# Token loads by single heads, scatters one at a time, and router logits in two places, in a convolution and expert-routing kernel

## The chip, the core and the metric

The kernel runs on one core of a Trainium2 chip. A core has five engines with queues of their own: TensorE (matmuls; the profile keeps its weight loads apart as PEld), VectorE (DVE), ScalarE (ACT), GpSimd (POOL) and SyncE (SP, which only issues transfers). Each engine works through its queue in program order and waits on semaphores where it needs another's result. Sixteen DMA engines carry all transfers, which SyncE, ScalarE and GpSimd issue. Matmuls write to PSUM banks, which ScalarE and VectorE empty.

The metric is the device time of one execution in microseconds (us), the median of several runs. Lower is better.

## What is computed

A causal convolution of seven taps, with softmax-normalised weights for each of eight heads of 24 channels, is followed by a mixture of eight experts. Each token's expert is the argmax of its logits, unless a local gate keeps the expert of the token before it, so the choice runs along the sequence. There are 8 sequences of 3584 tokens with 192 channels; an expert is 192 to 1024 to 192 with a relu. All is in float32.

```python
w = softmax(weight)                                   # [8 heads, 7 taps]
x = einsum('hk,bskhg->bshg', w, windows(x_pad))       # 24 channels to a head
logits = x @ w_gate                                   # [B, S, 8]
local_gate = sigmoid(x @ w_local)
for b in range(B):
    prev_e = -1
    for s in range(S):
        fresh_e = argmax(logits[b, s])
        e = fresh_e if s == 0 or local_gate[b, s] < 0.5 else prev_e
        prev_e = e
        p = softmax(logits[b, s])
        out[b, s] = p[e] * (relu(x[b, s] @ w1[e]) @ w2[e])
```

## The kernel before

**The pipeline.** Tokens are taken in groups. The groups are convolved, routed (logits, argmax, the run along the sequence, each token's place among the tokens of its expert) and scattered: each token's row of 195 words goes by an indirect DMA of GpSimd to its slot in DRAM (`slots`), where the tokens of one expert stand together. A scatter takes 128 rows. While later groups are on their way, *blocks* of tokens that are sure to be full are loaded back (`xg`), transposed, multiplied by their expert's two matrices and sent to the output by another indirect DMA (line 1198). Blocks of one tile (128 tokens) come first, 51 of them (numbers 0 to 50), then 20 pairs (51 to 70), then 31 quads of four tiles (71 to 101), then 14 single ones. Groups 0 and 1 go a special way at the start (`wide`, `wide_route`). Groups 2 and 3 hold 1792 tokens, the later ones 3584.

**Token loads and the filter.** A group is convolved in *units*, `(g, qq)`, of `DH = D // XQ` channels. With `XQ = 4` a unit is two heads. `load_x` (148) fetches a unit to one of three places in `x_all` for the small groups, or one of two for the large ones. ScalarE issues that transfer, except the first three, which SyncE issues. `tap` (417) multiplies one head's first tap on ScalarE (line 426) and `conv` (453) adds the other six on VectorE (line 464, six instructions a head). `taps` (438), called once in `output`, issues the next load if it is within the depth (3 or 2 units), then taps ahead for this unit and the next; `ready` (429) says whether the next may begin: its load was issued in an earlier block, and the groups whose buffer it will use have been routed and scattered.

**Order of the work.** The order of every engine is written out by hand (`manual_schedule`). The loop over blocks (1358) emits, for block i: `hidden` (first matrix, lines 1086 and 1090), or for quads `seven` (a scheme with seven products, line 1136), the next block's transposes (`turn_out` 1043, `turn_in` 1055), a `step`, `output` (second matrix, line 1178, its emptying on ScalarE 1186 and VectorE 1193, and the store 1198), and for smaller blocks a further `step`. `step(time, bank)` (1240) takes so much of the VectorE work that is waiting, from the routing (`route` 688) or else the filter. `ensure` (1304) issues the loads of rows up to three blocks ahead; it returns early where the group isn't routed and scattered, and in the last block before the need it works that off first. On SyncE's queue a load of rows waits for the scatters of its group, and the weights' loads stand in the same queue.

**Scatters.** `to_put` holds the scatters of routed groups; `put` (865) issues one, behind a given instruction. `more` (885) issues a second where the list is long, `puts_by` (890) both. They hang behind relus (1090), the copies of the transposes (1064) and copies in `seven`.

**Logits.** `logits` (642) transposes a group's rows on VectorE (652) and multiplies them by the gate's weights in 48 matmuls of both halves for every 14 tiles (line 665), with a yield "half" in the middle, in a PSUM bank that `step` was given. Copies by ScalarE (669) empty it. `step` stops the routing at "half" unless `whole` is set, which only `ensure` does.

**Quads.** `combine_w` (1097) makes four sums of the next quad's first matrix on GpSimd (1102 to 1105).

Of the kernel before, what the change touches and what calls it, by code (L numbers as in the profile page):

```python
# [17 lines left out]
P = 128  # L18
# [16 lines left out]
XQ = 4  # L35
# [74 lines left out]
def kernel(  # L110
# [32 lines left out]
    x_all = xs.tile([P, 2 * NX, DH], F32, name="x_sb")  # L143
# [4 lines left out]
    def load_x(u, queue=None):  # L148
        g, qq = UNITS[u]
        n, skip = (NT, g % PER * PT) if g < EARLY else (NS, 0)  # L150
        at = (u + 2) % 3 * (NT + HALO) if g < EARLY else (u + 1) % 2 * NX
        x_sb = x_all[:, at:at + n + HALO, :]
        src = x[g // PER, qq]
        win = bass.AP(tensor=src.tensor, offset=src.offset + skip * DH,
                      ap=[[n * DH, P], [1, (n + HALO) * DH]])
        (queue or nc.scalar).dma_start(out=x_sb.rearrange("p t d -> p (t d)"), in_=win)
        x_in[u] = x_sb
        x_at[u] = -1 if queue else st["block"]
# [256 lines left out]
    EACH = H // XQ  # L415

    def tap(u, j):

        if (u, j) in begun:
            return  # L420
        begun.add((u, j))
        g, qq = UNITS[u]
        if (qq, j) == (0, 0):
            got[g] = rows_in(g)
        h, n = qq * EACH + j, NT if g < EARLY else NS
        nc.scalar.activation(got[g][:, :, Y0 + h * GS:Y0 + (h + 1) * GS],  # L426
                             x_in[u][:, :n, j * GS:(j + 1) * GS], Act.Copy, scale=c[:, h, 0:1])

    def ready(u):

        if u >= len(UNITS) or u not in x_in or st["block"] <= x_at[u]:
            return False
        last = (UNITS[u][0] // PER - 3) * PER + 1
        if last < 0:
            last = UNITS[u][0] // PER - 2
        return st["routed"] >= last and not any(p[0] <= last for p in to_put)

    def taps(most):

        u = len(x_in)  # L440
        if u < len(UNITS):
            depth = 3 if UNITS[u][0] < EARLY else 2
            if u - depth <= st["unit"] - (st["cgen"] is not None):
                load_x(u)
        for u in (st["unit"], st["unit"] + 1):
            if u > st["unit"] and not ready(u):
                return
            for j in range(EACH):
                if u >= 0 and (u, j) not in begun and most:
                    tap(u, j)  # L450
                    most -= 1

    def conv(u):
        g, qq = UNITS[u]
        n = NT if g < EARLY else NS
        tap(u, 0)
        yield 0
        for j in range(EACH):
            h = qq * EACH + j
            cols = got[g][:, :, Y0 + h * GS:Y0 + (h + 1) * GS]  # L460
            if j + 1 < EACH:
                tap(u, j + 1)
            for k in range(1, KC):
                nc.vector.scalar_tensor_tensor(cols, x_in[u][:, k:k + n, j * GS:(j + 1) * GS],  # L464
                                               c[:, h, k:k + 1], cols, Alu.mult, Alu.add)
                yield 0.6 if n == NT else 1.0
# [418 lines left out]
    def more(behind, n=KT):  # L885

        if len(to_put) > (NT if n < KT else NT // 2):
            put(behind)

    def puts_by(behind):  # L890
        put(behind)
        more(behind)

# [181 lines left out]
    def hidden(n, wb, xT, shares=(1, 1)):  # L1075
# [3 lines left out]
        for two in range(2):  # L1079
# [11 lines left out]
            for _ in range(shares[two] if n == 2 else (0, sum(shares))[two]):  # L1091
                put(relu)
            if two and (n == 2 or st["block"] % 2):
                more(relu, n)
        return [hT]

    def combine_w(wb):


        wt = hp.tile([P, 3, 2 * P], F32, name="wt")  # L1100
        b11, b12, b21, b22 = [wb[:, k * 2 * P:(k + 1) * 2 * P] for k in range(4)]
        nc.gpsimd.tensor_tensor(wt[:, 1, :], b22, b12, op=Alu.subtract)  # L1102
        nc.gpsimd.tensor_tensor(b12, b12, b11, op=Alu.subtract)
        nc.gpsimd.tensor_tensor(wt[:, 0, :], b22, b12, op=Alu.subtract)
        nc.gpsimd.tensor_tensor(wt[:, 2, :], b21, wt[:, 0, :], op=Alu.subtract)
        return wt
# [13 lines left out]
    def seven(wb, wt, xT, xc, turn_next, weights_next):  # L1120
# [12 lines left out]
        def times(to, a, b, first=False):  # L1133
            for j in range(2):
                for half, rows in halves():
                    nc.tensor.matmul(to[:, half, j, :], lhsT=b[rows, j * P:(j + 1) * P],  # L1136
                                     rhs=a[rows, :], start=(first and j == 0), stop=True,
                                     skip_group_check=True)

        times(xb, a11, b11, True)  # L1140
        puts_by(nc.scalar.copy(h11, xb))
        times(yb, s1, t1, True)
        times(yb, a23, b32)
        puts_by(nc.scalar.copy(h22, yb))
        times(xb, s2, t2)
        nc.scalar.copy(h12, xb)
        times(wbk, a12, b21, True)
# [4 lines left out]
        times(xb, s3, t3)  # L1152
# [3 lines left out]
        times(yb, s5, b32)  # L1156
# [3 lines left out]
        times(xb, a23, b31)  # L1160
        nc.vector.tensor_tensor(h12, yb, h12, op=Alu.add)
        puts_by(nc.scalar.activation(h12, h12, Act.Relu))
# [3 lines left out]
    def output(n, wb, xg, hT, rows_next=None):  # L1166

        for part, h in enumerate(hT):
# [3 lines left out]
            for two in range(2):  # L1172
                for k in range(m):
                    for m_ in range(4):
                        side, j = m_ // 2, m_ % 2
                        f = side * 4 + two * 2 + j
                        for half, rows in halves():
                            nc.tensor.matmul(yps[:, half, k * D:(k + 1) * D],  # L1178
                                             lhsT=h[two][rows, side, j, k * P:(k + 1) * P],
                                             rhs=wb[rows, WA + f * D:WA + (f + 1) * D],  # L1180
                                             start=(two == 0 and m_ == 0 and k == 0),
                                             stop=(f == FK - 1), skip_group_check=True)
# [5 lines left out]
            if rows_next and part == 0:  # L1188
                taps(min(n, 2))
            step((1.3 if n > 1 or st["block"] else 0) if n < KT else SIDE[2 + part],  # L1190
                 wps_p if n < KT or part == 0 else None)
# [21 lines left out]
          "bank": None, "due": False, "over": 0}  # L1213
# [26 lines left out]
    def step(time, bank=None, whole=False):  # L1240

        start_route()
        start_conv()
        go = st["rgen"] is not None and not (st["due"] and bank is None)
        st["bank"], st["due"] = bank, st["due"] and not go
        time += st["over"]
        while time > 0:
# [11 lines left out]
            elif c == "half":  # L1259
                go = whole  # L1260
# [25 lines left out]
    load_x(0, nc.sync)  # L1286
    load_x(1, nc.sync)
    load_x(2, nc.sync)
# [15 lines left out]
    def ensure(i):  # L1304

        for j in range(len(xgs) + i, min(i + AHEAD + 1, len(blocks))):
            g = blocks[j][3]
            while st["routed"] < g or any(p[0] <= g for p in to_put):
                if j > i + (2 if blocks[i][1] == 1 else 1):
                    return  # L1310
                step(4.2, wps_p, True)
# [19 lines left out]
    puts_behind(mark["lt", 1], 3)  # L1331
# [7 lines left out]
    gather(1, ya, picks[1], range(9))  # L1339
    next(route1)  # L1340
    puts_behind(mark["nf", 1], 2)
    puts_behind(mark["rs", 1], 4)
    step(1.8)
    at = turn_out(blocks[0][1], xgs[0])
    xT, _ = turn_in(blocks[0][1], at)
    gather(1, ya, picks[1], range(9, NB))
    next(route1)
    step(2.4)
    xgs[1] = gathered(picks[1])
# [8 lines left out]
    for i, (_, n, _, _) in enumerate(blocks):  # L1358
# [8 lines left out]
        def weights_next():  # L1367
            return combine_w(wbs[i + 1]) if n_next == KT else None
# [3 lines left out]
        else:  # L1372
            hT = hidden(n, wbs[i], xT, (1, 1) if i else (0, 0))
            wt = weights_next()
            at = turn_next()
        if n_next:
            xT, copied = turn_in(n_next, at)
            if n == KT or (len(to_put) > NT // 2 and n == 2):
                puts_by(copied)
        xcs = []  # L1380

        def rows_next():
            if n_next == KT and not xcs:
                xcs.append(combine_x(xT))

        if n == 2:
            rows_next()
        step(2.4 if i == 0 else {1: 2.3, 2: 4.7, 4: SIDE[1]}[n], zps_p if n == KT else xps_p)
        output(n, wbs.pop(i), xgs.pop(i), hT, rows_next)
# [94 lines left out]
```

## Time and profile before

| | us |
|---|---|
| timed runs | 1338.44, 1326.51, 1338.53 (median 1338.44) |
| the profiled execution | 1377.82 |
| its span in the profile, first to last instruction | 1376.1 |
| TensorE busy in the span | 1307.0 |
| VectorE / ScalarE / GpSimd busy | 824.0 / 688.0 / 622.2 |
| mean granted TensorE clock | 0.984 of full |

How to read it. A group of instructions is named by its line, its engine and what it writes and reads: `PE L1178 MATMUL ps<-wb,h` is a matmul of line 1178 into a bank `ps`. In a timeline a row gives start and length in us, then the group, and in brackets how long the engine was idle before it and what ended that idle time. "issue" and "remote" there mean that the profile shows nothing that it waited for, or something outside the core's records. In the chain of waits, the instruction that ended last is followed back to what released it, again and again. The list of waits gives total us, number, and the longest. DMA share is the mean busy share of the sixteen DMA engines.

The stages in the span are: the start up to 54, single blocks up to about 381, pairs up to about 610, quads up to 1290, then the last single blocks. Two tables of the page show the DMA load by 40 slices of 34.4 us:

```
DMA  5898899899787676674334442423342332332583
GB/s 179 327 342 312 322 352 331 316 316 349 295 327 257 216 242 235 213 282 142 124 139 145 144 139 83 151 100 115 134 151 88 133 128 93 128 119 85 189 315 114
```

### The profile page before, as it was taken

Reading aid. Unit: us, or ns where it says so; the run is one execution under the profiler, and the core shown is the slowest. Engines: PE = TensorE matmul, PEld = TensorE weight load, DVE = VectorE, ACT = ScalarE, POOL = GpSimd, SP = SyncE. Lnnn points to the kernel's source line nnn. Section 1 sums busy time; section 2 is a strip of 40 time slices with the busy share of each in tenths; the row PEclk is TensorE's granted clock in tenths of the full one; section 3 lists DMA queues with packets and bytes.
Section 4 is the critical chain, followed back from the end, with each engine's and each line's share of the span. In section 5 each row is a group of like instructions: output and inputs, shape, how many; then the busy total and the mean of one; then the engine's idle time right before and its main releaser. Section 6 shows DMA issues by size and latency. Waiting matters only on the chain.

```text
span 1376.1 us, 40772 instructions
## 1 busy us (share of the span) xinstructions
PE 1307.0 (95%) x16674; PEld 1256.1 (91%) x16674; DVE 824.0 (60%) x1891; ACT 688.0 (50%) x1402; POOL 622.2 (45%) x650
## 2 busy tenths in 40 slices
PE   9899889998899999998999999998999999999997
PEld 7889888998899998987998999888999999999997
DVE  6878687787787887887777755763333333343100
ACT  5355445554444444545564545443545645655453
POOL 4444444156366374476546643465543333333111
PEclk9999999999999999999999999999999999999999
DMA  5898899899787676674334442423342332332583
GB/s 179 327 342 312 322 352 331 316 316 349 295 327 257 216 242 235 213 282 142 124 139 145 144 139 83 151 100 115 134 151 88 133 128 93 128 119 85 189 315 114
DMA packets 62788, 281.17 MB, mean 204 GB/s; under 512 B 12032, under 2 KB 30647, under 8 KB 48258
## 3 DMA queue, kind: packets, MB, share of 16 engines
q1 hardware_dynamic: 36096, 210.76, 43.0%
q0 software_dynamic: 22320, 45.22, 9.0%
q10 hardware_dynamic: 4178, 22.51, 4.6%
q8 instruction: 134, 2.20, 0.6%
q14 instruction: 60, 0.49, 0.1%
HBM read 232.85 MB, written 46.07 MB: 203 GB/s over the span
## 4 chain that ended last, share of the span: by engine, by line
PE 85%; DVE 5%; DMA 5%; issue 3%; POOL 1%; ACT 1%; another core or an unknown queue 0%; DVEq 0%; POOLq 0%; ACTq 0%; SPq 0%
PE ps L1178 42%; PE ps L1136 21%; PE ps L1086 17%; DMA x_sb<-in_x_dram 3%; PE ps L665 2%; PE ps L400 2%; DVE y_sb L464 1%; DMA slots<-y_sb,posi 1%; DVE h L1153 1%; PE hps L249 1%; POOL slots L872 1%; DMA out_dram<-o_sb,xg 0%; PE hps L194 0%; ACT h L1090 0%
## 5 line engine op out<-in xcount | busy, mean ns | idle before, releaser
L1178 PE MATMUL ps<-wb,h 64*128 64x192 f32 x7328 | 641.4, 328 | 27.6 <-ACT h L1090 12.6
L1178 PEld LDWEIGHTS ps<-wb,h 64*128 64x128 f32 x7328 | 609.5, 189 | 37.7 <-ACT h L1090 19.9
L1198 POOL DMA_INDIRECT out_dram<-o_sb,xg x229 | 251.9, 1100 | 470.4 <-DVE o_sb L1193 397.3
L464 DVE SCALAR_TENSOR_TENSOR y_sb<-x_sb,c,y_sb 128x672 f32<-128x672 f32 (+1 forms) x384 | 322.7, 848 | 35.2 <-ACT y_sb L426 21.4
L872 POOL DMA_INDIRECT slots<-y_sb,posi x228 | 253.8, 1113 | 120.5 <-issue 52.8
L1086 PE MATMUL ps<-xT,wb 64*128 64x128 f32 (+1 forms) x4080 | 299.3, 298 | 3.5 <-issue 2.1
L1193 DVE SCALAR_TENSOR_TENSOR o_sb<-ps,xg,o_sb 128x192 f32<-128x192 f32 x229 | 87.7, 413 | 353.2 <-ACT o_sb L1186 346.8
L1086 PEld LDWEIGHTS ps<-xT,wb 64*128 64x128 f32 x4080 | 281.5, 188 | 16.1 <-issue 7.2
L1186 ACT ACTIVATE o_sb<-ps,xg 128x192 f32<-128x192 f32 x229 | 87.3, 418 | 332.0 <-PE ps L1178 286.9
L1090 ACT ACTIVATE h<-ps 128x256 f32<-128x256 f32 (+1 forms) x340 | 127.5, 431 | 152.3 <-PE ps L1086 109.5
L1064 ACT COPY xT<-ps 128x128 f32<-128x128 f32 (+2 forms) x464 | 194.3, 419 | 10.5 <-issue 3.2
L1136 PE MATMUL ps<-xT,wb 64*128 64x256 f32 x1488 | 182.8, 379 | 1.1 <-issue 1.0
L1136 PEld LDWEIGHTS ps<-xT,wb 64*128 64x128 f32 x1488 | 157.9, 189 | 7.6 <-issue 2.9
L1150 DVE TENSOR_TENSOR h<-ps,h 128x1024 f32<-128x1024 f32 x31 | 37.9, 1223 | 92.8 <-PE ps L1136 90.0
L1102 POOL TENSOR_TENSOR wt<-wb 128x256 f32<-128x256 f32 x31 | 23.5, 758 | 129.1 <-issue 129.1
L1136 PE MATMUL ps<-xc,wt 64*128 64x256 f32 x496 | 67.7, 381 | 1.6 <-issue 1.6
L1151 ACT ACTIVATE h<-h 128x1024 f32<-128x1024 f32 x31 | 32.8, 1057 | 69.4 <-DVE h L1150 50.2
L400 PE MATMUL ps<-ident,xg 64*64 64x64 f32 (+1 forms) x916 | 51.2, 220 | 11.0 <-DVE h L1150 4.7
L426 ACT ACTIVATE y_sb<-x_sb,c 128x672 f32<-128x672 f32 (+1 forms) x64 | 48.9, 793 | 24.2 <-DMA x_sb<-in_x_dram 24.1
L1136 PE MATMUL ps<-xc,wb 64*128 64x256 f32 x496 | 60.0, 376 | 0.0
L400 PEld LDWEIGHTS ps<-ident,xg 64*64 64x64 f32 (+1 forms) x916 | 46.3, 125 | 14.9 <-issue 6.6
L1136 PEld LDWEIGHTS ps<-xc,wt 64*128 64x128 f32 x496 | 53.3, 189 | 4.1 <-issue 2.4
(266 smaller groups left out, 975.1 us busy)
## 6 DMA issues: line engine op xcount, KB each, us to landing
wb<-in_w_dram SPq DMA_DIRECT2D x112, 1536.0 KB
x_sb<-in_x_dram ACTq DMA_DIRECT2D x24, 816.0 KB
xg<-slots SPq DMA_DIRECT2D x31, 390.0 KB
wb<-in_w_dram SPq DMA_DIRECT2D x12, 512.0 KB
xg<-slots SPq DMA_DIRECT2D x63, 97.5 KB
xg<-slots SPq DMA_DIRECT2D x20, 195.0 KB
out_dram<-o_sb,xg POOLq DMA_INDIRECT x229
slots<-y_sb,posi POOLq DMA_INDIRECT x228
```

The lines of the kernel that those rows point to most:

```text
L400: nc.tensor.transpose(to, src[rows], identity=ident[rows, rows])
L426: nc.scalar.activation(got[g][:, :, Y0 + h * GS:Y0 + (h + 1) * GS], x_in[u][:, :n, j * GS:(j + 1) * GS], Act.Copy, scale=c[:, h, 0:1])
L464: nc.vector.scalar_tensor_tensor(cols, x_in[u][:, k:k + n, j * GS:(j + 1) * GS], c[:, h, k:k + 1], cols, Alu.mult, Alu.add)
L872: ins = nc.gpsimd.indirect_dma_start(out=slots[:, :], in_=rows, in_offset=None, out_offset=bass.IndirectOffsetOnAxis(ap=to, axis=0)).ins
L1064: copied = nc.scalar.copy(a, b)
L1086: nc.tensor.matmul(hps[:, half, j, :], lhsT=wb[rows, f0:f0 + P], rhs=xT[rows, d, :], start=(d == 0 and j == 0), stop=(d == KD - 1), skip_g ...
L1090: relu = nc.scalar.activation(hT[two][:, half], hps[:, half], Act.Relu)
L1136: nc.tensor.matmul(to[:, half, j, :], lhsT=b[rows, j * P:(j + 1) * P], rhs=a[rows, :], start=(first and j == 0), stop=True, skip_group_che ...
L1178: nc.tensor.matmul(yps[:, half, k * D:(k + 1) * D], lhsT=h[two][rows, side, j, k * P:(k + 1) * P], rhs=wb[rows, WA + f * D:WA + (f + 1) * ...
L1186: nc.scalar.activation(o_sb[:, k, :], yps[:, 0, k * D:(k + 1) * D], Act.Copy, scale=xg[:, at + k, 0:1])
L1193: nc.vector.scalar_tensor_tensor(o_sb[:, k, :], yps[:, 1, k * D:(k + 1) * D], xg[:, at + k, 0:1], o_sb[:, k, :], Alu.mult, Alu.add)
L1198: sent = nc.gpsimd.indirect_dma_start(out=out, in_=o_sb[:, k, :], in_offset=None, out_offset=bass.IndirectOffsetOnAxis(ap=xg.bitcast(I32)[ ...
```

## The change

- **Loads.** `XQ` becomes `H`: a unit is one head of 24 channels, loaded by itself. `x_all` holds the same number of words, as six places for the small groups and four for the large. SyncE loads the first four units. `taps` issues up to `most` loads in a call, to a depth of six units, then three to five, then four. It taps up to three units ahead, and where blocks are single only units whose load was issued two blocks ago.
- **Scatters.** `more` and `puts_by` go. In `hidden` each relu of a pair, and the last relu of a single block, is followed by one scatter (a second for long lists, in odd blocks). In quads six scatters hang behind matmuls: four in `seven`, two in `output` (by `between`). The four sums of `combine_w` become four steps between them.
- **Logits.** The step in `output` no longer gives a bank, so a group's products begin in the step before the output. Half of them are made there, and the other half at the start of the next step (`st["half"]`), unless the bank is `wps_p`, where both are made together.
- **The first blocks.** Two steps of filter work before block 0 become one of 0.6, that of block 0 falls from 2.4 to 0.6; block 1's tokens are gathered in one go ahead of the rest of group 1's routing; the rows of block 2 are transposed after block 1's output, not before it. Numbers of scatters behind the early marks change.
- `ensure` takes filter and routing steps only while the group isn't routed.

The diff, cut to its core:

```diff
-XQ = 4
+XQ = H
-    x_all = xs.tile([P, 2 * NX, DH], F32, name="x_sb")
+    x_all = xs.tile([P, 4 * NX, DH], F32, name="x_sb")
-        at = (u + 2) % 3 * (NT + HALO) if g < EARLY else (u + 1) % 2 * NX
+        at = (u + 2) % 6 * (NT + HALO) if g < EARLY else u % 4 * NX
...
-    def ready(u):
+    def ready(u, wait=1):
-        if u >= len(UNITS) or u not in x_in or st["block"] <= x_at[u]:
+        if u >= len(UNITS) or u not in x_in or st["block"] < x_at[u] + wait:
...
-    def taps(most):
-        u = len(x_in)
-        if u < len(UNITS):
-            depth = 3 if UNITS[u][0] < EARLY else 2
-            if u - depth <= st["unit"] - (st["cgen"] is not None):
-                load_x(u)
-        for u in (st["unit"], st["unit"] + 1):
-            if u > st["unit"] and not ready(u):
+    def taps(most, wait):
+        for _ in range(most):
+            u = len(x_in)
+            if u == len(UNITS):
+                break
+            depth = 6 if UNITS[u][0] < EARLY else max(3, 21 - u) if u < 19 else 4
+            if u - depth > st["unit"] - (st["cgen"] is not None):
+                break
+            load_x(u)
+        for u in range(max(st["unit"], 0), st["unit"] + 4):
+            if u > st["unit"] and not ready(u, wait):
                 return
...
-    def more(behind, n=KT):
-        if len(to_put) > (NT if n < KT else NT // 2):
-            put(behind)
-    def puts_by(behind):
-        put(behind)
-        more(behind)
...
-            for _ in range(shares[two] if n == 2 else (0, sum(shares))[two]):
+            if shares and (n == 2 or two or st["block"] % 2 and len(to_put) > NT):
                 put(relu)
-            if two and (n == 2 or st["block"] % 2):
-                more(relu, n)
...
-        puts_by(nc.scalar.copy(h11, xb))
+        nc.scalar.copy(h11, xb)
...
-        times(wbk, a12, b21, True)
+        put(times(wbk, a12, b21, True))
...
-        times(xb, s3, t3)
+        put(times(xb, s3, t3))
...
-        times(yb, s5, b32)
+        put(times(yb, s5, b32))
         at = turn_next()
         times(xb, a22, t4)
         wt = weights_next()
-        times(xb, a23, b31)
+        next(wt)
+        put(times(xb, a23, b31))
+        next(wt)
...
-                taps(min(n, 2))
-            step((1.3 if n > 1 or st["block"] else 0) if n < KT else SIDE[2 + part],
-                 wps_p if n < KT or part == 0 else None)
+                taps(min(n, 2), 2 if n == 1 else 1)
+            step((1.3 if n > 1 or st["block"] else 0) if n < KT else SIDE[2 + part])
...
+        if st["half"]:
+            st["half"] = False
+            route_op()
...
             elif c == "half":
-                go = whole
+                go = st["bank"] is wps_p
+                st["half"] = not go
...
-                step(4.2, wps_p, True)
+                if st["routed"] < g:
+                    step(4.2, wps_p)
                 put()
...
-    gather(1, ya, picks[1], range(9))
+    gather(1, ya, picks[1], range(NB))
     next(route1)
-    puts_behind(mark["nf", 1], 2)
     puts_behind(mark["rs", 1], 4)
-    step(1.8)
     at = turn_out(blocks[0][1], xgs[0])
     xT, _ = turn_in(blocks[0][1], at)
-    gather(1, ya, picks[1], range(9, NB))
+    xgs[1] = gathered(picks[1])
     next(route1)
-    step(2.4)
-    xgs[1] = gathered(picks[1])
+    step(0.6)
...
-        if n_next:
+        if n_next and i != 1:
             xT, copied = turn_in(n_next, at)
-            if n == KT or (len(to_put) > NT // 2 and n == 2):
-                puts_by(copied)
+            if n < KT and len(to_put) > (0 if n == 1 else NT // 2):
+                put(copied)
...
+        def between(part, two, k, ins):
+            if n == 2 and (two, k) == (1, 0) and len(to_put) > NT // 2:
+                put(ins)
+            if n == KT and part == 0 and two != k:
+                put(ins)
+                if k:
+                    next(wt)
...
-        step(2.4 if i == 0 else {1: 2.3, 2: 4.7, 4: SIDE[1]}[n], zps_p if n == KT else xps_p)
+        step(0.6 if i == 0 else {1: 2.3, 2: 4.7, 4: SIDE[1]}[n], zps_p if n == KT else xps_p)
...
+        if i == 1:
+            xT, _ = turn_in(n_next, turn_next())
```

## Prediction

> **What bounds the kernel now.** I read the page top first (busy shares, clock), then the stages (windows of 50 us), then the order of TensorE's instructions with the idle time before each, then the chain of waits around the larger gaps, and last GpSimd's and SyncE's queues around them.
>
> ```profile
> span 1376.1 us, 40772 instructions
> PE 1307.0 (95%) x16674; PEld 1256.1 (91%) x16674; DVE 824.0 (60%) x1891; ACT 688.0 (50%) x1402; POOL 622.2 (45%) x650
> ...
> PE 85%; DVE 5%; DMA 5%; issue 3%; POOL 1%; ACT 1%; another core or an unknown queue 0%; DVEq 0%; POOLq 0%; ACTq 0%; SPq 0%
> ```
> TensorE is the bound, and its work is the same before and after (the built programs hold the same matmuls, differently ordered). So only its waiting can move. The 50 us windows give its idle time by stage, in us: 5.8 in 0-50, 28.0 in 50-400 (single-tile blocks), 2.3 in 400-600 (pairs), 22.9 in 600-1000 (quads, while routing lasts), 0.4 in 1000-1350, 9.7 in the tail, which no edit touches.
>
> ```profile
> 154.71 4.52 PE L1178 MATMUL ps<-wb,h 64*128 64x192 f32 x32 [5.39 <-DVE o_sb L1193]
> 206.88 5.49 PE L1178 MATMUL ps<-wb,h 64*128 64x192 f32 x32 [3.88 <-ACT h L1090]
> 240.39 2.87 PE L1178 MATMUL ps<-wb,h 64*128 64x192 f32 x32 [1.84 <-ACT h L1090]
> 321.89 4.55 PE L1178 MATMUL ps<-wb,h 64*128 64x192 f32 x32 [4.74 <-ACT h L1090]
> ```
> These four gaps are over half of the 28 us. The instruction after a long one also takes 4.5 to 5.5 us where undisturbed ones take 2.66: the granted clock falls to 0.86 in the windows 150-175 and 200-225. What ScalarE waited for is in its own list and in the chain:
>
> ```profile
> ACT y_sb L426 <- DMA x_sb<-in_x_dram: 24.1, 10, 5.0
> ```
> ```profile
> 141.93 8.70 DMA x_sb<-in_x_dram
> 195.84 9.84 DMA x_sb<-in_x_dram
> 230.64 8.55 DMA x_sb<-in_x_dram
> 308.91 11.02 DMA x_sb<-in_x_dram
> ```
> The first tap of a unit (line 426) stands in ScalarE's queue one block, 5.45 us, after its own load was issued there; the load takes 8.6 to 11.0 us; every relu (line 1090) behind it waits, and TensorE with it.
>
> In the quads the gaps are of another kind. Four windows show when:
>
> ```profile
> 700.00:785.00 85.00, 80.01 (x866) 76.46 (x864) 60.89 (x111) 42.74 (x58) 54.28 (x52) 0.98 0.43 146
> 785.00:880.00 95.00, 94.56 (x1223) 89.71 (x1222) 61.08 (x138) 51.37 (x74) 38.14 (x40) 1.00 0.32 110
> 880.00:980.00 100.00, 89.39 (x936) 84.66 (x934) 45.43 (x128) 44.73 (x60) 58.13 (x63) 0.98 0.37 126
> 980.00:1080.00 100.00, 99.24 (x1124) 98.77 (x1122) 33.67 (x57) 55.44 (x73) 40.90 (x46) 1.00 0.37 126
> ```
> The columns are length, then busy time and count of TensorE matmul, weight load, VectorE, ScalarE, GpSimd, then clock, DMA share, GB/s. TensorE loses 5.0 and 10.6 us where GpSimd issues 52 and 63 instructions, and 0.4 and 0.8 us where it issues 40 and 46. The timeline shows four to eight indirect DMAs 1.27 us apart (887.38, 888.65, 889.92, 891.18) and then TensorE, VectorE and ScalarE all idle, with no releaser ("issue", "remote").
>
> **The change, part by part.** Its own time for the profiled run is 1377.8 us, 1.7 around the span; the median of the timed runs is 1338.4, which is 39 less. Back-to-back work in this trace is 54 us of start, 50 single blocks of 5.45, 20 pairs of 10.66, 31 quads of 20.42, 14 singles, 26 of logits (1.9% of the chain) and 9.7 of tail: 1285. The profiled run stands 91 above that, the timed ones 1338 - 1.7 - 1285 = 52. So I count a gain from a latency wait at 52/91 = 0.57 in the timed runs.
>
> *Loads by single heads* (lines 35, 151, 438-451). 64 loads of half the size replace 32. In the built order of ScalarE's queue the distance from a load to its first tap is one block for most units before, and two blocks or more for 31 of the 34 single heads that ScalarE loads while single blocks run after (10.9 us against a transit of 8.6 to 11.0 for twice the bytes). The four gaps sum to 15.9 us; 2.5 of the last are a wait on an output store, which stay. The slow instructions behind three of them cost (4.52 + 5.49 + 4.55) - 3 x 2.66 = 6.6. Three more gaps of 0.46 to 0.49 come behind two taps in a row, which become single ones: 1.4. Together 21; I take 20, since the load side tightens a little. The added 32 issues cost 32 x 0.335 = 11 us of ScalarE's queue, which is 50% busy, at the place after the output copy; the relu behind that place still waits for its matmuls after it, 1.0 us in the mean (109.5 us in 109 waits on line 1086), so none is counted. VectorE does the same 672 half-steps. The Trainium skill speaks against this part: "DMA: Bandwidth & Descriptors", Rules for kernel authors, wants at least 1 MiB in one DMA, and its fit (Anatomy of one DMA) is 2.0 us plus bytes over 436 GB/s, an estimate of 3.9 us for 816 KB and 2.9 for 408 KB. By it a whole-unit load would be there within the 5.45 us and this part would be worth 0 or, with 32 more fixed costs on a shared path, less. The trace has 8.6 to 11.0 us at a DMA share near 0.9, so the row decides: 20.
>
> *Scatters one by one* (885-892, 1091-1094, 1141-1162, new places behind matmuls). Same 228 scatters; quads carry six each, about 2 us apart, instead of up to eight in fours. What the quads lose now in the two windows with bursts is 15.6 us, against under 1 where GpSimd issues less. Gain between 0 and 15.6. The skill's "Runtime: NRT & Kernel Launch", Instruction fetch mechanics, says that crossing a fetch boundary is "mostly hidden", which would make gaps with all engines idle and no releaser unrelated to scatters, and this part 0. The two quiet windows, with as much code in them, are nearer: 15. The weight sums (1102-1105) are split into four steps between scatters, and are done a block ahead of their use: nothing, as long as scatters don't hold them up by more than that.
>
> *What slower scattering costs.* The rule that doubled scatters for a long queue goes, so a group is finished about a block later; SyncE's queue shows five gathers of rows moved behind a weight load. Where the next group's first block comes soon, its rows are late. Block 51 is worst: block 49 begins with five scatters left where before one was. Before:
>
> ```profile
> 370.60 0.96 POOL L872 DMA_INDIRECT slots<-y_sb,posi  x1 [0.30 <-issue]
> ...
> 373.07 1.24 SPq L1026 DMA_DIRECT2D xg<-slots  x2
> ...
> 376.74 0.40 PE L400 MATMUL ps<-ident,xg 64*128 64x64 f32 x8
> ```
> The rows were just in time. Four more scatters at 1.27 us put the last at 375.7; landing 2.5 later as here, and 3.0 for the gather (86.27 to 89.27 at block 7), make 381.2, 4.5 late; with the 7.6 us that a scatter took at 78.40 it is 9.6, and 1.9 of slow clock follows. I take 6.5. Behind it SyncE's queue holds the next weights. Block 62 (the twelfth pair) gets its group's last scatter after block 60's two stores; by the pair at 598.08 (stores at 601.88 and 603.38, turn at 603.26) rows would be there at 604.7 + 2.5 + 3 = 610: between 0 and 7 late, I take 5. Block 21: 1. Waits of 0.7 and 1.2 at 372 and 378 go with the routing work that moves away: -1.9. Sum 10.6; the late transits shrink in timed runs, so 9 there.
>
> *Logits in two places.* Half of a group's products now fill the wait for the relu, the rest follow the output, into the bank that the next block's first products use. Those then wait for two copies, 0.54 us in the two places where it is so now; some six places after: 3 lost, 1 regained by filling. -2.
>
> *The first unit.* Ten half-steps of the filter (0.57 us each) leave VectorE's queue ahead of the first routing; seven gathers go ahead of the transpose that TensorE waits 1.9 us for (40.85); block 1 turns the next rows after its output. Gain 1.9 there, the 1.7 at 64.12 (VectorE behind), and 1.3 of the 2.4 at 89.41, since scatter 24 becomes the first of its block: 5. What was moved is done by block 8 (62 half-steps against 61) in slack of VectorE.
>
> Sum in the profiled execution: 20 + 15 + 5 - 10.6 - 2 = 27, so 1350. In the timed runs: 0.57 x 35 = 20, + 5 - 9 - 2 = 14: **1324**.
>
> **The rivals.** *Slower: the late group.* If a scatter takes 7.6 us to land at the group ends, blocks 51 and 62 lose 9.6 and 10 us, each with 1.9 of slow clock, and blocks 7 and 21 some 3: 27. If moreover the timed runs show none of the waits of 35 us (they are 39 shorter than the profiled one), the sum is 1338 + 27 + 2 - 5 = 1362. It decides from the point where the last scatter lands over 4 us after its issue and the x waits in timed runs are under 15 us. For it: 89.41, which is such a wait already. Against: 373.07.
>
> *The DMA engines become the bound.* In 50-400 they are 89% busy at 326 GB/s; in the window 225-250 they reach 0.98 at 380. Freed of its waits TensorE asks for 114 MB in 325 us, 351 GB/s, share about 0.95; weights would come late instead of x, and half of the x gain is lost: 1330. Against: 100-125 and 275-300 run TensorE at 24.9 and 25.0 of 25 with shares of 0.89 and 0.93.
>
> *It doesn't do what it says: gaps stay.* If the bursts don't make the idle time, or the profiler's own traffic does, the quad part is 0 and the sum 1324 + 8.6 = 1333, no change.
>
> *More than forecast.* All the latency waits are in the timed runs too, at full size: 1338 - 27 = 1311; and 1300 where blocks 51 and 62 get their rows in time.
>
> **How the numbers follow.** A measurement of this kernel tells 1% (13 us: its three runs span 12) from no change. Chances: the forecast 0.42 (1312 to 1332), more than forecast 0.18, DMA bound 0.13, gaps stay 0.14, late group 0.13. Faster by over 1% means below 1325.1: about 0.6 of the forecast's own chance, all of the second, a fifth of the two middle ones: 0.49, which I round to 0.50. Slower (above 1351.8): 0.13 of the late group, and 0.03 for mishaps in the others: 0.16. Within 1%: 0.34. The range runs from 1301 (the far end of the second case) to 1350, which leaves out most of the late group.
>
> **What would show it.** Right: no wait of line 426 on x loads above 2 us before 400 us; no gap with all engines idle after four scatters between 700 and 980; a gap of 4 to 10 us before line 400's transposes at block 51. Wrong: x waits that have turned into waits on weights; the quad gaps there although scatters are apart; gaps at blocks 51 and 62 longer than 10 us.

## The result, and the profile after

| | before | after |
|---|---|---|
| timed runs, median (range), us | 1340.27 (1326.51 to 1357.8) | 1329.09 (1327.5 to 1333.16) |
| ratio, 95% interval | | 0.9936 [0.9916, 0.9956] |
| span of the profile | 1376.1 | 1328.4 |

The change saves 0.6%: less than the 1% named in the prediction as the line to "no change", and 5 us less than the 1324 forecast. First the head of the page of the kernel after, with the shares of the chain of waits:

```profile
span 1328.4 us, 40894 instructions
PE 1283.2 (97%) x16674; PEld 1232.9 (93%) x16674; DVE 826.5 (62%) x1891; ACT 692.1 (52%) x1402; POOL 621.0 (47%) x650
...
PE 87%; DMA 5%; DVE 3%; ACT 2%; issue 1%; POOL 1%; ACTq 0%; SPq 0%; POOLq 0%; DVEq 0%
```

TensorE has the same 16674 matmuls. The profiled spans differ by 47.7 us where the timed medians differ by 11.2; the runs on the second kind of chip, below, bear on why. After, span and timed runs agree.

What ScalarE waited for, from the list of waits of the kernel after (total us, number, longest):

```profile
ACT y_sb L425 <- DMA x_sb<-in_x_dram: 0.5, 1, 0.5
```

Before, this was 24.1 us in 10 waits. The loads part does what it says. So do the quads, from the windows of the kernel after (length, busy time and count of TensorE, weight loads, VectorE, ScalarE and GpSimd, clock, DMA share, GB/s):

```profile
700.00:850.00 150.00, 148.92 (x1838) 141.84 (x1836) 104.09 (x192) 81.42 (x112) 86.13 (x84) 1.00 0.40 136
850.00:960.00 110.00, 110.00 (x1254) 103.83 (x1252) 64.49 (x179) 58.93 (x81) 63.39 (x68) 1.00 0.39 133
```

TensorE loses 1.1 us in 260. In the same windows of the kernel before it lost 15.0:

```profile
700.00:850.00 150.00, 144.57 (x1732) 137.31 (x1730) 97.48 (x171) 76.09 (x106) 82.03 (x80) 0.99 0.39 134
850.00:960.00 110.00, 100.44 (x1086) 95.26 (x1084) 64.12 (x195) 51.62 (x71) 57.17 (x62) 0.98 0.34 115
```

What is new stands in TensorE's list of waits:

```profile
PE ps L1074 <- ACT ls L666: 11.5, 10, 1.8
PE ps L400 <- DMA xg<-slots: 8.8, 4, 4.7
PE ps L1170 <- ACT ls L666: 3.8, 4, 1.8
PE ps L1074 <- ACT xT L1052: 3.3, 1, 3.3
```

15.3 us are waits for the copies that empty the logits' bank (line 666), 8.8 for rows of tokens, 3.3 for the transposed tokens of block 2. Before, the first two were:

```profile
PE ps L1086 <- ACT ls L669: 1.1, 2, 0.5
PE ps L400 <- DMA xg<-slots: 2.4, 1, 2.4
```

The new waits in TensorE's timeline (start, length, group, idle before):

```profile
60.68 4.75 PE L1074 MATMUL ps<-xT,wb 64*128 64x128 f32 x48 [3.33 <-ACT xT L1052]
...
351.27 0.45 PE L400 MATMUL ps<-ident,xg 64*128 64x64 f32 x8 [2.61 <-DMA xg<-slots]
...
448.60 5.45 PE L1074 MATMUL ps<-xT,wb 64*128 64x256 f32 x48 [1.78 <-ACT ls L666]
...
480.06 0.69 PE L400 MATMUL ps<-ident,xg 64*128 64x64 f32 x8 [4.67 <-DMA xg<-slots]
```

Rows two and four are blocks 51 and 62, the late group of the prediction. Row three is its logits term, and why it is larger than thought shows on ScalarE's queue ahead of it:

```profile
446.00 0.42 ACT L1180 ACTIVATE o_sb<-ps,xg 128x192 f32<-128x192 f32 x1 [3.74 <-PE ps L1170]
446.06 0.34 ACTq L156 DMA_DIRECT2D x_sb<-in_x_dram  x1
446.32 0.41 ACT L1180 ACTIVATE o_sb<-ps,xg 128x192 f32<-128x192 f32 x1
446.62 1.61 ACT L425 ACTIVATE y_sb<-x_sb,c 128x672 f32<-128x672 f32 x2
448.13 0.42 ACT L666 COPY ls<-ps 128x128 f32<-128x128 f32 x2
```

Two evacuations, a load's issue and two taps stand ahead of the two copies, and the next hidden matmuls need the copies' bank.

### The profile page after: what moved, and what is told of

Read it like the earlier page. It is cut to its first block, busy times and chain, and to the rows that moved or that the text cites. A ratio compares the mean times of both kernels' runs of the same rounds, so it can differ in the third digit from the quotient of the medians.

```text
span 1328.4 us, 40894 instructions
## 1 busy us (share of the span) xinstructions
PE 1283.2 (97%) x16674; PEld 1232.9 (93%) x16674; DVE 826.5 (62%) x1891; ACT 692.1 (52%) x1402; POOL 621.0 (47%) x650
## 4 chain that ended last, share of the span: by engine, by line
PE 87%; DMA 5%; DVE 3%; ACT 2%; issue 1%; POOL 1%; ACTq 0%; SPq 0%; POOLq 0%; DVEq 0%
PE ps L1170 43%; PE ps L1125 22%; PE ps L1074 18%; DMA slots<-y_sb,posi 2%; PE ps L400 2%; DMA wb<-in_w_dram 1%; PE ps L662 1%; DMA xg<-slots 1%; DVE y_sb L461 1%; ACT y_sb L425 1%; DMA out_dram<-o_sb,xg 1%; PE hps L249 1%; PE hps L194 0%; PE yps L630 0%; POOL slots L869 0%
## 5 line engine op out<-in xcount | busy, mean ns | idle before, releaser
L1170 PE MATMUL ps<-wb,h 64*128 64x192 f32 x7328 | 626.6, 326 | 5.0 <-ACT ls L666 3.8
L1170 PEld LDWEIGHTS ps<-wb,h 64*128 64x128 f32 x7328 | 600.7, 188 | 9.8 <-ACT ls L666 4.9
L1074 PEld LDWEIGHTS ps<-xT,wb 64*128 64x128 f32 x4080 | 278.8, 190 | 28.4 <-ACT ls L666 14.2
L1125 PE MATMUL ps<-xT,wb 64*128 64x256 f32 x1488 | 178.5, 378 | 0.0
L1125 PEld LDWEIGHTS ps<-xT,wb 64*128 64x128 f32 x1488 | 150.5, 188 | 9.2
L1125 PE MATMUL ps<-xc,wt 64*128 64x256 f32 x496 | 65.0, 378 | 2.1 <-issue 2.1
L649 DVE STREAM_TRANSPOSE z<-y_sb 128x768 f32<-128x768 f32 (+1 forms) x56 | 45.5, 852 | 22.6 <-PE ps L662 22.5
L400 PE MATMUL ps<-ident,xg 64*64 64x64 f32 (+1 forms) x916 | 47.4, 219 | 9.4 <-DMA xg<-slots 8.8
L400 PEld LDWEIGHTS ps<-ident,xg 64*64 64x64 f32 (+1 forms) x916 | 42.7, 124 | 14.8 <-issue 5.0
L1125 PEld LDWEIGHTS ps<-xc,wt 64*128 64x128 f32 x496 | 50.4, 188 | 6.2 <-issue 2.5
```

The costliest lines, as they stand in the source:

```text
L400: nc.tensor.transpose(to, src[rows], identity=ident[rows, rows])
L649: nc.vector.transpose(z[:, t:u, :], y_sb[:, part * NT + t:part * NT + u, Y0:Y0 + D])
L1074: nc.tensor.matmul(hps[:, half, j, :], lhsT=wb[rows, f0:f0 + P], rhs=xT[rows, d, :], start=(d == 0 and j == 0), stop=(d == KD - 1), skip_g ...
L1125: ins = nc.tensor.matmul(to[:, half, j, :], lhsT=b[rows, j * P:(j + 1) * P], rhs=a[rows, :], start=(first and j == 0), stop=True, skip_gro ...
L1170: ins = nc.tensor.matmul(yps[:, half, k * D:(k + 1) * D], lhsT=h[two][rows, side, j, k * P:(k + 1) * P], rhs=wb[rows, WA + f * D:WA + (f + ...
```

## The experiments

The runs fell on chips of two kinds, told apart by the time of the kernel before. On the first kind it takes 1338 to 1340 us; the first four runs are from one such chip, and the result above is counted there by its time, since its chip isn't recorded. On the second kind (two chips) it takes 1391. Each chip was used in one session only, so no run tells whether the chip makes the difference or something else that held for the session; "kind of chip" stands for either. Ratios are always to the kernel before in the same session.

### First kind: each part taken away, and the loads alone

**The loads alone.** The kernel before, with this part of the change (and the taps that go with it):

```diff
-XQ = 4
+XQ = H
-        at = (u + 2) % 3 * (NT + HALO) if g < EARLY else (u + 1) % 2 * NX
+        at = (u + 2) % 6 * (NT + HALO) if g < EARLY else u % 4 * NX
-    def taps(most):
+    def taps(most, wait):
+        for _ in range(most):
...
+            depth = 6 if UNITS[u][0] < EARLY else max(3, 21 - u) if u < 19 else 4
...
+            load_x(u)
+        for u in range(max(st["unit"], 0), st["unit"] + 4):
+            if u > st["unit"] and not ready(u, wait):
```

> The kernel before with the loads alone changed (single heads, six and four places, taps two blocks behind a load). If the late token loads were the chief loss: no wait of the first tap on a load over 2 us before 400 us, 1318 to 1328 us, and times that spread less than those of before. If the DMA engines are the bound in the first 400 us: the waits go over to weights and rows, 1335 us or more. If the scatter bursts and the first blocks carried the gain: 1338 to 1342.

Measured: 1322.1 us (1318.92 to 1322.53), 0.9869 [0.9835, 0.9902]. This part alone saves 16.6 us and beats the full change (interval 0.9916 to 0.9956). The runs spread over 3.6 us where those of before spread over 18.0. One tap waits longer than the 2 us expected: 2.9 at 87 us.

**All but the loads.** The full change with the old loads: the edit above, reversed.

> The changed kernel with the old loads (two heads a unit, three and two places). If the loads carry the gain: 1338 to 1352 us with a wide spread, and gaps of 2 to 5 us of TensorE behind the first tap. If the scatters or the order of the first blocks carry it: within 3 us of 1329.

Measured: 1363.05 us (1357.36 to 1367.48), 1.0175 [1.0136, 1.0215]. The other three parts without the loads make the kernel 24 us slower, which is outside both expectations. ScalarE's list of waits of this run:

```profile
ACT y_sb L426 <- DMA x_sb<-in_x_dram: 33.8, 12, 4.6
```

So with old loads such waits can be larger on the first kind of chip (33.8 us) than in the profile of before (24.1). The kernel before itself was not profiled there.

**Old scatters.** The full change with the scatters and weight sums as before:

```diff
-            if shares and (n == 2 or two or st["block"] % 2 and len(to_put) > NT):
-                put(relu)
+            for _ in range(shares[two] if n == 2 else (0, sum(shares))[two]):
+                put(relu)
+            if two and (n == 2 or st["block"] % 2):
+                more(relu, n)
...
-        put(times(wbk, a12, b21, True))
+        times(wbk, a12, b21, True)
...
```

> The changed kernel with the old places of the scatters (bursts, doubled for long lists) and the weight sums in one piece. If bursts make the gaps with all engines idle in the quads: these come back between 600 and 960 us, 5 to 15 us in sum, 1334 to 1342 us. If those gaps came from elsewhere: no gaps, and 1325 to 1330.

Measured: 1331.38 us (1327.33 to 1332.88), 0.9945 [0.9921, 0.997], not to be told from the full change. TensorE's timeline at blocks 51 and 62:

```profile
349.12 0.45 PE L400 MATMUL ps<-ident,xg 64*128 64x64 f32 x8 [2.40 <-DMA xg<-slots]
...
475.62 0.69 PE L400 MATMUL ps<-ident,xg 64*128 64x64 f32 x8 [4.14 <-DMA xg<-slots]
```

The late rows are there with the old scatters too. In the traces, the group that block 51 needs gets its last logits in block 49 both here and in the full change (at 342 and 344 us), and block 49 begins with five or six scatters to go. With the loads alone the last logits are in block 47 (335 us), and one scatter is left. The logits are late, and the scatters follow them. And the quads have no gaps although the bursts are back, with up to twelve indirect DMAs in a row: TensorE is busy 148.92 of 150 and 110.00 of 110 us between 700 and 960.

**Old logits.** The full change with the logits in one place:

```diff
-            step((1.3 if n > 1 or st["block"] else 0) if n < KT else SIDE[2 + part])
+            step((1.3 if n > 1 or st["block"] else 0) if n < KT else SIDE[2 + part],
+                 wps_p if n < KT or part == 0 else None)
...
-                go = st["bank"] is wps_p
-                st["half"] = not go
+                go = whole
...
-                if st["routed"] < g:
-                    step(4.2, wps_p)
+                step(4.2, wps_p, True)
```

> The changed kernel with the logits in the old place and bank. If the two places cost what the changed profile shows as waits on the copies of the logits (15 us): those waits fall under 3 us in sum and the time to 1313 to 1320 us. If the halves that fill the wait for the relu give as much back: 1326 to 1332.

Measured: 1327.45 us (1324.73 to 1329.07), 0.9906 [0.9871, 0.994]. The waits on copies fall from 15.3 to 6.7 us, those on rows from 8.8 to 1.7, with none ahead of blocks 51 and 62:

```profile
PE ps L1074 <- ACT ls L666: 3.9, 4, 1.8
PE ps L1170 <- ACT ls L666: 2.8, 2, 1.8
PE ps L400 <- DMA xg<-slots: 1.7, 2, 1.5
```

But only 1.6 us of time is gained (0.3%, or 4 us, by the ratios), with overlapping intervals. In their place this run has waits of 5.6 us for block 2's tokens, 5.0 for an output bank (o_sb), 5.0 for relus and 3.4 at the first quad.

Where the loads alone gain on the full change is seen in the same windows of both. Loads alone:

```profile
60.00:100.00 40.00, 33.14 (x554) 32.16 (x552) 32.43 (x67) 18.56 (x57) 15.83 (x16) 0.96 0.91 344
...
250.00:350.00 100.00, 98.19 (x1632) 95.88 (x1632) 82.90 (x202) 55.54 (x168) 52.97 (x44) 1.00 0.92 350
350.00:450.00 100.00, 98.20 (x1260) 94.67 (x1261) 85.50 (x206) 48.48 (x105) 56.68 (x46) 1.00 0.78 274
450.00:540.00 90.00, 90.00 (x1168) 84.08 (x1166) 76.22 (x176) 44.34 (x96) 50.49 (x42) 1.00 0.71 248
```

The full change:

```profile
60.00:100.00 40.00, 38.34 (x599) 37.96 (x603) 32.95 (x62) 23.34 (x71) 18.53 (x19) 0.96 0.95 356
...
250.00:350.00 100.00, 94.49 (x1646) 91.79 (x1642) 80.58 (x191) 53.88 (x163) 54.13 (x45) 1.00 0.90 339
350.00:450.00 100.00, 95.54 (x1204) 88.64 (x1206) 76.25 (x161) 45.77 (x99) 47.00 (x39) 0.98 0.75 261
450.00:540.00 90.00, 83.97 (x998) 79.41 (x1002) 72.12 (x163) 38.16 (x82) 49.44 (x42) 0.96 0.67 228
```

The full change, with its new first unit, wins 5.2 us between 60 and 100. From 250 to 540, where the logits' copies and the late rows fall, TensorE is idle 16.0 us in the full change and 3.6 with the loads alone.

### Second kind: one part added to the loads

The next three add one part each to the loads. The first unit:

```diff
-        gather(1, ya, picks[1], range(9))
+        gather(1, ya, picks[1], range(NB))
...
-            at = turn_next()
-        if n_next:
+            at = turn_next() if i != 1 else None
+        if n_next and i != 1:
...
+        if i == 1:
+            xT, _ = turn_in(n_next, turn_next())
```

> The kernel before with the new loads and the new order of the first unit; scatters and logits as before. Theory A (the parts add up): from 1322.1 for the loads alone, 1331.4 without the scatters, 1327.5 without the logits and 1329.1 for all, the first unit's order is +7.7, the scatters -2.3, the logits in two places +1.6. Then this run gives about 1330, and its profile has the gap of 3 to 6 us ahead of block 2's first hidden matmul (waiting for the transposed tokens copied behind a tap on ScalarE). Theory B (the logits' copies cost, the first unit's order is what was forecast, at most -2 to +5 with its gains): 1320 to 1327, and less than 1327 without the logits' two places. The line between them is 1327.

The scatters (the full change's `put` behind each matmul group, `between`, and `combine_w` in four steps):

> The kernel before with the new loads and the scatters spread; first unit and logits as before. Theory A (the parts add up): -2.3 to the loads' 1322.1, so about 1320, with no gap of all engines in the quad blocks, as the run with the loads alone had none either. Theory B (forecast: spreading brings up to 15 in the quads and costs 10 ahead of blocks 51 and 62): 1317 at best, 1327 to 1332 if only the late scatters are left of it. The profile tells: waits for gathered tokens of 2.6 and 4.7 us ahead of blocks 51 and 62, or not.

The logits (the diff of "Old logits", reversed):

> The kernel before with the new loads and the logits in two places; first unit and scatters as before. Theory A (the parts add up): +1.6 to the loads' 1322.1, so about 1324, the 15 us of waits for logits copies being paid mostly by time that other waits of the old place lose. Theory B (these waits cost what they last): 1322 + 10 to 15 = 1332 to 1337. The forecast's own term was -2 to -3: 1319 to 1320.

The kernel before, profiled again:

> The kernel before, profiled a second time. Theory A: the gaps of all engines in the quad blocks of the first profile (15.6 us between 700 and 960) belong to that one execution, whose span of 1376 was 38 above the median: this profile has fewer than 4 us of them between the same blocks, and a span between 1327 and 1350. Theory B (the forecast's): they belong to the bursts of scatters, and this profile has at least 10 us of them again.

Here the kernel before took 1391.24 us and its profile a span of 1390.1, so the expected microseconds don't apply, only the ratios. Loads with the first unit: 1.0026 [1.0004, 1.0048]. Loads with the scatters: 0.9686 [0.9646, 0.9725]. Loads with the logits: 1.0049 [1.0028, 1.0069]. The profile of the kernel before had the gaps in the quads again. Its windows around one of them:

```profile
717.50:720.00 2.50, 0.80 (x16) 0.66 (x16) 0.82 (x2) 1.06 (x1) 0.96 (x1) 1.00 0.72 237
720.00:722.50 2.50, 1.33 (x9) 1.15 (x8) 2.46 (x4) 1.27 (x2) 0.00 (x0) 0.66 0.01 3
722.50:725.00 2.50, 2.50 (x18) 2.23 (x18) 2.29 (x12) 1.04 (x2) 1.44 (x2) 0.65 0.02 7
```

and TensorE's timeline in them:

```profile
718.27 0.57 PE L400 MATMUL ps<-ident,xg 64*128 64x64 f32 x12 [0.91 <-issue]
719.77 0.32 PE L400 MATMUL ps<-ident,xg 64*64 64x64 f32 x4 [0.93 <-issue]
721.27 2.08 PE L1136 MATMUL ps<-xT,wt 64*128 64x256 f32 x8 [1.17 <-DVE h L1153]
```

Eight indirect DMAs of GpSimd run from 706.8 to 718.5. At their end TensorE stops three times within 5 us, twice for nothing that the profile shows, and then works at a clock of 0.65 to 0.66: eight matmuls take 2.08 us that take 1.13 elsewhere. A low clock does not follow every stop: after one of 1.22 us at 762 eight matmuls take 1.13. In the whole profile there are 44 such waits on "issue", 23.1 us. Theory B's number held (TensorE loses 15.7 us between 700 and 960, and the span is far above theory A's), its cause only in part: on the first kind such bursts have no gaps.

Set against the loads alone on the other chip of this kind (0.9988, next section), the parts cost +0.4% (first unit), -3.0% (scatters) and +0.6% (logits). Theory A's additive steps from the first kind were +0.6, -0.2 and +0.1%. Theory B asked, in the same order, for at most +0.4, at best -0.4, and +0.8 to +1.1%. So the first unit decides nothing, the scatters went far beyond both theories, and the logits lie between the two, nearer to B.

### Second kind: the loads alone, the full change and two versions side by side

> The kernel before with the new loads alone, a second time, beside the full change. Theory A (whether the gaps of all engines come with the bursts of scatters is a matter of the chip): where they do not come (before at about 1338), 0.987 of before, quads 700 to 960 without gaps, and 7 us faster than the full change; where they do (before at about 1391), at least 10 us of gaps between the quad blocks, 0.99 to 1.0 of before, and slower than the full change. Theory B (the gaps came with other parts of those kernels, the bursts have none): 0.987 on either, and no gaps on either.

> The full change, beside the loads alone on one chip. Theory A: on a chip where the bursts have no gaps 0.994 of before, as at first; where they have, 0.965 to 0.975, since its spread scatters take the gaps away (the run of loads and scatters was 0.9686 there). Theory B: 0.994 on either.

> New loads and spread scatters, the logits and the first unit as before, beside the full change. Theory A (the logits in two places are what delays the tokens of blocks 51 and 62, and their copies hold up the hidden matmuls): at least 7 us faster than the full change on either kind of chip, no wait for gathered tokens ahead of blocks 51 and 62. Theory B (the spread scatters delay them, as forecast): within 3 us of the full change.

The last moves the second half of the logits to the front of what follows the output's matmuls:

```diff
+            if st["half"]:
+                st["half"] = False
+                route_op()
             o_sb = op.tile([P, HU, D], F32, name="o_sb")
```

> The full change with one difference: the two copies of the logits (and the bookkeeping behind them) are placed ahead of the evacuation, the loads and the taps on ScalarE's queue, right behind the logits' matmuls. Theory A (the copies' place on the queue is what the 15.3 us of waits measure): these waits fall below 4 us, and the time by 6 to 12 us against the full change. Theory B (another wait takes their place, as removing the second place altogether brought only about 2): within 3 us of the full change, with the output or the taps waiting in their stead.

| kernel | us | ratio, 95% interval |
|---|---|---|
| before | 1391.08 | |
| loads alone | 1388.5 | 0.9988 [0.996, 1.0017] |
| full change | 1352.46 | 0.9724 [0.9695, 0.9752] |
| loads and scatters | 1346.74 | 0.9685 [0.9642, 0.9728] |
| full change, copies early | 1348.59 | 0.9699 [0.9668, 0.9731] |

The order is turned round: the loads alone, best on the first kind, bring nothing here that is clear of the interval, and the scatters bring 42 us on top of them. That part also splits the weight sums into four steps, and no run separates the two. The same kernel, loads alone, in its quads. On the first kind:

```profile
700.00:850.00 150.00, 148.92 (x1834) 141.01 (x1832) 100.26 (x210) 81.53 (x113) 77.82 (x79) 1.00 0.39 134
850.00:960.00 110.00, 110.00 (x1260) 106.77 (x1258) 48.59 (x115) 62.98 (x83) 71.35 (x79) 1.00 0.43 147
```

and on the second:

```profile
700.00:850.00 150.00, 142.12 (x1710) 135.39 (x1708) 91.71 (x166) 73.38 (x104) 83.22 (x81) 0.99 0.36 122
850.00:960.00 110.00, 102.64 (x1079) 96.03 (x1078) 63.86 (x195) 54.91 (x73) 53.87 (x59) 0.97 0.38 126
```

One program loses 1.1 us there and 15.2 here. With the scatters added, on the second kind, the gaps are gone from these windows:

```profile
700.00:850.00 150.00, 148.49 (x1828) 139.79 (x1826) 102.16 (x186) 81.39 (x112) 85.42 (x85) 1.00 0.40 137
850.00:960.00 110.00, 110.00 (x1248) 105.07 (x1246) 63.31 (x176) 59.76 (x80) 64.14 (x70) 1.00 0.42 144
```

They are not gone everywhere: this run still has 34 waits on "issue" (11.1 us), the full change here 26 (12.3 us), most of it before 600. Of the 37.6 us between the spans of loads alone (1384.4) and loads with scatters (1346.8), 18.6 is idle time of TensorE and 19.0 is longer busy time of the same matmuls (1317.0 against 1298.0). The mean clock, 0.983 against 0.991, makes at most some 11 of the 19.0, an estimate from the spans times what the clocks lack to 1; the rest isn't explained.

The theories on the chips: A held. The full change's 0.9724 lies inside its bounds, loads alone are at 0.9988, and the gaps are there. The theories on the late rows: loads with scatters are 5.7 us faster than the full change, where A asked for at least 7 and B for at most 3, and the intervals overlap. But that run has no wait for rows at blocks 51 and 62, as A said, although its scatters are spread.

The early copies met neither theory. The waits for them fell from 13.9 us (full change on this chip) to 7.5, not below 4, and the longest from 1.8 to 0.6. The time fell by 3.9, within what the intervals leave open.

No version that was run is best on both kinds. Loads with scatters was not run on the first, the early copies not either.

## Why the prediction was right or wrong

**The outcome.** The measured time lies 5 us from the forecast and well inside its range. The favoured outcome, faster by over 1% (0.50), did not come; within 1% (0.34) did.

**The bound and the loads: right.** The waits booked on x loads fell from 24.1 to 0.5 us (3.2, if two waits of taps that the profile books on a weight load, 2.7 us, are really on x). The term of 20 measured 16.6 alone on the first kind, and some 32 with the other parts present (1.0175 less 0.9936, of 1338.65); in that kernel without the new loads the waits on loads are 33.8. The rule of the Trainium skill that was weighed there ("DMA: Bandwidth & Descriptors", Rules for kernel authors: at least 1 MiB in a transfer) would have given 0 or less; the measurement decides against it. The page's fit, weighed with it, is for transfers that GpSimd issues, and these are ScalarE's. On the second kind the part brought 2.6 us, inside its interval: TensorE's gain between 150 and 250 (98.12 busy against 86.64) was lost again between 45 and 100 and around the first quad.

**The scaling by 0.57: wrong.** The prediction laid the 39 us between profile and timed runs on latency waits and shrank all of them. For the loads that makes 0.57 x 20 = 11.4, and alone on the first kind they saved 16.6. What the profile of before has and those of the first kind have not is the gaps without a releaser: 41 waits on "issue", 20.2 us, against 1 to 3 waits and 0.7 to 4.8 us in the full change and the four runs there, and 44 and 23.1 for the kernel before on the second kind. Its 1377.8 is also longer than any timed run set beside the change (at most 1357.8). That it came from a chip of the second kind is the likely reading, not a shown one: on that kind the fastest timed run of before is 1378.5.

**The scatters' 15: on the wrong kind.** On the first kind no profiled kernel has the gaps, not even with the old scatters, and the term is 0 within the intervals (0.9945 against 0.9936). On the second kind it is 42 (1388.5 to 1346.7), of which idle time is about half. "Mostly hidden", as the Trainium skill has it of instruction fetch ("Runtime: NRT & Kernel Launch", Instruction fetch mechanics), fits the first kind; the gaps of the second speak neither for nor against it. The transfers of instructions are 134, 2.20 MB, at a share of 0.6 or 0.7% on either. In the trace of before on the second kind they take 1.05 us in the mean, and between 700 and 960 the 12 waits on "issue" of 0.4 us or more (9.2 us) overlap with them for 0.3: around the stop at 717 to 721 one starts at 707.8 and the next at 723.6. So TensorE hardly stopped while such a transfer ran; whether it stopped for one not yet begun stays open.

**The late group's 10.6: near in size, wrong in cause.** Blocks 51 and 62 waited 2.6 and 4.7 us, where 6.5 (a wait of 4.5 and slow clock) and 5 were taken; the first is below the 4 to 10 named as a sign. But the old scatters keep these waits and the old logits take them away, and spread scatters with the old logits have none: the second place puts a group's last logits later. The step "what slower scattering costs" should have been booked on the logits.

**The logits' -2: mis-sized.** Six places at 0.54 us were counted, from the two places where a copy came right behind its matmuls. There were 14, at 1.1 in the mean, since the copies stand behind evacuations, an issue and taps. Not all of it is this part's: with the old logits 6.7 of the 15.3 us remain. With the rows (8.8 to 1.7), the part holds 15.7 us of waits. Much of that time would be spent on other waits: taking the part out gained 1.6, while adding it to the loads cost about 8.5 on the second kind (1.0049 against 0.9988, on two chips).

**The first unit's +5: right only against the loads alone.** Between 45 and 100 TensorE is busy 4.9 us more than with the loads alone, but only 1.5 more than before. Not foreseen was the 3.3 us at block 2: its turned rows are copied by ScalarE (line 1052) only behind a tap that waited 2.2 us.

```profile
59.90 0.58 ACT L425 ACTIVATE y_sb<-x_sb,c 128x336 f32<-128x336 f32 x1 [2.20 <-DMA wb<-in_w_dram]
60.38 1.19 ACT L1052 COPY xT<-ps 128x128 f32<-128x128 f32 x4
```

Added to the loads alone on the second kind, the part cost about 5 (1.0026 against 0.9988; the intervals overlap).

**The sum: near by luck.** 1324 against 1329.09: the loads gave about what 0.57 x 35 gave, because a gain that was taken at half size stood in for one of the scatters that wasn't there. The rest, +5 - 9 - 2 = -6 forecast, came out as -7 (1322.1 to 1329.1; -9 by the ratios), with its terms wrongly shared out. The rivals: the DMA engines didn't become the bound (share 0.99 at 384 GB/s between 150 and 250, with TensorE busy 97.8 of 100). "Gaps stay" fails too: there were none on the first kind, and on the second they left the quads between 700 and 960.

## What to carry to other kernels

Before a wait in a profile is scaled, ask whether the profile and the times come from the same chip and session: a profile that stands outside the range of its timed runs needs a second profile first. An edit that splits work into a second place puts the copy that frees its bank at a new place on another engine's queue; price it by what stands ahead of it there, not by the copy's own length. Where several edits go together, time each against the one that carries the gain: here one part alone was better than all four on one kind of chip, and another part carried nearly all of the gain on the other.

## What was not expected of the hardware

Two kinds of chip ran one program (loads alone) at 1322.1 and 1388.5 us, 5% apart, with 1.1 us in 2 and 19.1 us in 43 waits on "issue". The difference in span, 67.2, is 29.0 idle and 38.2 longer busy time, of which the mean clocks (0.995 and 0.983) make at most some 17 by the same estimate. What makes the gaps, and whether it is the chip or the session, stays open.
